# Eleven microseconds planned for weight loads decoded within attention, seven for the first MoE's, and part of two chunks' moves issued by GpSimd

## Chip, cores and metric

The kernel runs on one core of a Trainium2 chip. The metric is the device time of one execution in microseconds (us). A comparison is made with the median of several executions.

## What is computed

Talking-heads attention (scores and attention weights are mixed over the heads, before and after the softmax), then a mixture-of-experts layer with one dense expert and an ELU (the first MoE), then a second one with a SoLU and a layer norm. All weights of both MoEs arrive as 64-bit floats and are used as 32-bit ones.

```python
scores = scale * np.matmul(q, k.transpose(0, 1, 3, 2))      # 4 batches, 12 heads, 448 x 448, head size 64
scores = np.einsum('bhij,hg->bgij', scores, w_pre)
attn = np.exp(scores - np.max(scores, axis=-1, keepdims=True))
attn = attn / (np.sum(attn, axis=-1, keepdims=True) + 1e-09)
attn = np.einsum('bhij,hg->bgij', attn, w_post)
x = np.matmul(attn, v)                                      # 1792 tokens x 768
h = x @ w_in                                                # 768 -> 2048
g = np.where(h > 0.0, h, np.exp(np.minimum(h, 0.0)) - 1.0)
x = g @ w_out                                               # 2048 -> 768
h = x @ w_in2                                               # 768 -> 1024, SoLU, layer norm, 1024 -> 768
```

## The kernel before, in words

**Attention.** A batch's 448 query rows are cut into chunks of up to 12 groups of ten rows (`CH`, 17 chunks in all; the first batch's are 4, 8, 12, 12 and 9 groups). For each chunk PE makes the scores of two heads at a time (L445), ACT or DVE copies them from PSUM into one of eight `sev` buffers (L451), and a DMA, called a move here (`move`, L453), spreads each head's rows into `sp`, where twelve heads of five rows lie on 64 partitions. There is one `sp` buffer for even chunks and one for odd. Two groups of a chunk form a unit; there are 92. A unit is the mixing before the softmax on PE (`pre`, tile `pm`, L515), the row maximum on DVE (L520), the exponential with its sum on ACT (L525), 1/sum on DVE (L529, L532), the weights of the second mixing on GpSimd (L536), that mixing on PE (`post`, tile `po`, L548) and its copy from PSUM on DVE or ACT (L556). At the end of each chunk PE multiplies with v (tile `av`, L597).

**Weights decoded within attention.** The first MoE works on groups of 256 hidden columns (`fg`, eight of them). The weights of group 0 are decoded while attention runs, in 16 pieces of 192 columns (L616 to L664): a load of 64-bit words into `kst` (two buffers), then on DVE the clamp of the high words (L635), on ACT the scaling (L639), on DVE three integer steps (L643, L647, and the join, L652), and a store into `w1s` in DRAM. A piece's load depends on the join of the piece before. Near the end of attention six loads `wy <- w1s` (`add_w`, L683) bring them back and split them.

**What sets the order of attention.** Each operation is an entry of a list with a rank, its engine or engines with a cost each, and what it depends on. `schedule` (L298) works through the list with a clock of its own: an operation may start when each of its inputs is `seen`. That is the input's planned end plus `lag` where a lag is given, and otherwise plus the engine's `tail` and `more`:

```python
            if o.lag is not None:
                return o.end + o.lag
            ...
            return o.end + tail[o.eng] + o.more
```

For a DMA on SP the tail is 2.0, so a `kst` load with `more=.3` counts as landed 2.3 us after its issue, and a `wy` load with `more=.5` after 2.5 us. Where several engines are named, the one that would end first is taken. The clock only sets the order in which instructions are written into each engine's stream. On the chip every stream runs in order, and each instruction waits for its real inputs.

**The first MoE.** For every group `fg` and each of four token blocks `tb`, `hid` makes two halves `ft` (L258), `elu` brings them through DVE, ACT and DVE (L265, L266, L267), and `outp` makes six PSUM tiles `o` in four buffers (L750), which DVE adds to `x1` (L766). The weights of group `fg + 1` and, in what room is left, those of the second MoE (`w2_spill`) are decoded meanwhile. `decode` (L156) gives a piece's stages with the time that must pass before each:

```python
        first = [(0, load, 0), (3.3, hiword, 1, 2), (0, loword, 1), (0, sign, 1), (0, join, 1)]
```

`load` is a 512 KB DMA into `ws` (L163), `hiword` is L172 on DVE and L173 on ACT, `loword`, `sign` and `join` are L177, L182 and L186 on DVE; a split on ACT and GpSimd follows (L189, L190). `tick` (L95) is called behind every half of `hid` and every tile of `outp`, and writes stages whose time has come by a second clock, `clk`, which `spend` moves on. At most three pieces are active, and at most two of them past `load`. `w1_piece(fg, i)` decodes piece `i` of group `fg`; pieces 0 to 2 are of `w_in`, 3 to 5 of `w_out`.

Of the kernel before, what the change touches and what calls it, by code (L numbers as in the profile page):

```python
# [64 lines left out]
def kernel(ctx: ExitStack, tc: tile.TileContext, qa, kt, vt, wpre, wpost,  # L65
# [4 lines left out]
    nc = tc.nc  # L70
# [82 lines left out]
    x_done = [[] for _ in range(NB)]  # L153
    w1, xT, xst_t, wi_t, wo_t = {}, {}, {}, {}, {}

    def decode(src, n, mul=None, dst=None, spill2=None):  # L156

        a = {}

        def load():  # L160
            p = pools["wstg"]
            a["t"] = (p.tile([128, 1024], F32, tag="ws", name="ws", bufs=4)[:, :2 * n],)
            nc.sync.dma_start(out=a["t"][0].bitcast(U64), in_=src)  # L163

        def hiword():
            p = pools["wstg"]
            a["t"] += (p.tile([128, 512], F32, tag="wy", name="wy")[:, :n],
                       p.tile([128, 512], I32, tag="wq", name="wq")[:, :n])
            st, y, q = a["t"]
            a["y"] = y  # L170
            w = st.rearrange("p (n t) -> p n t", t=2)
            nc.vector.tensor_scalar(w[:, :, 1], w[:, :, 1], F64_TOP, -F64_TOP, ALU.min, ALU.max)  # L172
            nc.scalar.activation(out=y, in_=w[:, :, 1], func=AF.Copy, scale=2.0 ** -112)  # L173

        def loword():
            wi = a["t"][0].rearrange("p (n t) -> p n t", t=2).bitcast(I32)
            nc.vector.tensor_scalar(a["t"][2], wi[:, :, 0], 29, None, ALU.logical_shift_right)  # L177

        def sign():
            wi = a["t"][0].rearrange("p (n t) -> p n t", t=2).bitcast(I32)  # L180
            q = a["t"][2]
            nc.vector.scalar_tensor_tensor(q, wi[:, :, 1], -0x80000000, q, ALU.bitwise_and, ALU.bitwise_or)  # L182

        def join():
            y, q = a["t"][1].bitcast(I32), a["t"][2]
            nc.vector.scalar_tensor_tensor(y, y, 3, q, ALU.logical_shift_left, ALU.bitwise_or)  # L186

        def split():
            nc.scalar.copy(dst[0], a["y"])  # L189
            nc.gpsimd.tensor_tensor(dst[1], a["y"], f(dst[0]), ALU.subtract)  # L190

        def split2():
            t = a["t"][0].bitcast(F32R)
            hi, lo = t[:, :n], t[:, n:]
            if mul is not None:
                nc.scalar.mul(a["y"], a["y"], mul)
            nc.scalar.copy(hi, a["y"])
            nc.gpsimd.tensor_tensor(lo, a["y"], f(hi), ALU.subtract)

        def store2():  # L200
            nc.sync.dma_start(out=spill2, in_=a["t"][0])

        first = [(0, load, 0), (3.3, hiword, 1, 2), (0, loword, 1), (0, sign, 1), (0, join, 1)]
        if spill2 is not None:
            return first + [(SD, split2, SW), (1.8, store2, 0)]
        return first + [(SD, split, SW)]
# [4 lines left out]
    def w1_piece(fg, i):  # L211

        m, sl = i // 3, slice((i % 3) * 512, (i % 3) * 512 + 512)
        return decode((wo1 if m else wi1)[fg, :, sl], 512, dst=(w1[fg][2 * m][:, sl], w1[fg][2 * m + 1][:, sl]))

    def xT_alloc(tb, p):
        xT[tb] = (p.tile([128, ECH, S], F32R, name=f"xh{tb}"), p.tile([128, ECH, S], F32R, name=f"xl{tb}"))
# [157 lines left out]
    for u in range(NU):  # L375
# [4 lines left out]
        c = units[u][0]  # L380
# [18 lines left out]
    k_op, q_op, av_op, sc_ev = {}, {}, {}, {}  # L399

    def dma(out, in_, e="sp"):
        (nc.scalar if e == "act" else nc.sync).dma_start(out=out, in_=in_)


    pool("spb")
# [24 lines left out]
    def add_score(c, h):  # L430

        b, _, G = CH[c]
        n = 5 * G
        ring = ("sc", "po", "pm")[h // 2 % 3] if c == 0 else "sc"
        scb, svb = [Buf(ring) for _ in range(2)], [Buf("sev") for _ in range(2)]
        r = t_sc[c, h]
        key = "sc", c, h

        def mm(e):
            T[key] = [pools["ps_" + ring].tile([128, 512], F32, tag=ring, name="sc") for _ in range(2)]  # L440
            q, k = q_t[c, h // 6], kt_t[b, h]
            for x in range(2):
                for i in range(2):
                    sl = slice(64 * i, 64 * i + 64)
                    nc.tensor.matmul(T[key][i][64 * x:64 * x + 64, :S], q[sl, h % 6 // 2, 64 * x:64 * x + 64], k[sl, :],  # L445
                                     start=True, stop=True)

        def evac(e, i):
            t = T["sv", c, h + i] = (k0.tile([128, S], F32, name=f"s0_{h + i}") if c == 0 else
                                     sev_p.tile([128, S], F32, tag="sev", name="sev"))  # L450
            copier(e)(t, T[key][i][:, :S])  # L451

        def move(e, i, p, r0, r1):  # L453
            if c not in sp_t:
                sp_t[c] = sp_t[c - 2]
            dma(sp_t[c][p:p + 13 * (r1 - r0 - 1) + 1:13, 0:G, :], T["sv", c, h + i][r0 * G:r1 * G], e)

        o1 = op(r, mm, [k_op[b, h], q_op[c, h // 6]], scb, [qb_[c, h // 6], kb[b, h]], pe=SC)
        for i in range(2):
            sv = [] if c == 0 else [svb[i]]  # L460
            o2 = sc_ev[c, h + i] = op(r + .9 + .1 * i, lambda e, i=i: evac(e, i), [o1], sv, [scb[i]], act=.54, dve=.62)
            for n, to in enumerate([(h + i, 0, 10)] if h + i < 11 else [(11, 0, 5), (64, 5, 10)]):
                sp_op.setdefault(c, []).append(op(r + 2 + .2 * i + .1 * n, lambda e, i=i, to=to: move(e, i, *to), [o2], [spb_[c]], sv, lag=3.5, sp=.78, **({"act": .78} if c < 2 else {})))

    spb_ = {c: Buf(f"sp{(NC - c) % 2}") for c in range(NC)}
    o = op(7.0, lambda e: dma(wpre_t, wpre), sp=.5)
# [148 lines left out]
    last = None  # L615
    for n in range(16):  # L616
        sl = slice((n % 8) * 192, (n % 8) * 192 + 192)
        src, dst = (wo1 if n > 7 else wi1)[0, :, sl], w1s[n // 8][:, sl]
        t0 = t_pre[first[2]] + 10 + n * (t_pre[first[NC - 1]] - t_pre[first[2]] - 35) / 16
        sb = Buf("kst")  # L620
        key = ("w", n)

        def load(e, key=key, src=src):
            t = kst_p.tile([128, 2, S], F32, tag="kst", name="kst").rearrange("p a b -> p (a b)")
            T[key] = t[:, 0:384], t[:, 384:576], t[:, 576:768].bitcast(I32)
            dma(T[key][0].bitcast(U64), src)

        def words(key=key):
            st, y, q = T[key]
            w = st.rearrange("p (n t) -> p n t", t=2)  # L630
            return w, w.bitcast(I32), y, q

        def clamp(e, words=words):
            w = words()[0]
            nc.vector.tensor_scalar(w[:, :, 1], w[:, :, 1], F64_TOP, -F64_TOP, ALU.min, ALU.max)  # L635

        def scale(e, words=words):
            w, _, y, _ = words()
            nc.scalar.activation(out=y, in_=w[:, :, 1], func=AF.Copy, scale=2.0 ** -112)  # L639

        def loword(e, words=words):
            _, wi, _, q = words()
            nc.vector.tensor_scalar(q, wi[:, :, 0], 29, None, ALU.logical_shift_right)  # L643

        def sign(e, words=words):
            _, wi, _, q = words()
            nc.vector.scalar_tensor_tensor(q, wi[:, :, 1], -0x80000000, q, ALU.bitwise_and, ALU.bitwise_or)  # L647

        def join(e, words=words):
            _, _, y, q = words()  # L650
            y = y.bitcast(I32)
            nc.vector.scalar_tensor_tensor(y, y, 3, q, ALU.logical_shift_left, ALU.bitwise_or)  # L652

        def store(e, key=key, dst=dst):
            dma(dst, T[key][1])

        o = op(t0, load, [last], [sb], sp=.5, more=.3)
        o = op(t0 + 4, clamp, [o], [], [sb], dve=.17)
        oa = op(t0 + 4.5, scale, [o], [], [sb], act=.26)
        o = op(t0 + 5, loword, [o], [], [sb], dve=.17)  # L660
        o = op(t0 + 5.5, sign, [o], [], [sb], dve=.27)
        o = op(t0 + 6, join, [oa, o], [], [sb], dve=.27)
        T["ws", n] = op(t0 + 6.5, store, [o], [], [sb], sp=.5, more=.3)
        last = o  # L664
# [18 lines left out]
    def add_w(i, r):  # L683
        m, sl = i // 3, slice((i % 3) * 512, (i % 3) * 512 + 512)
        wy = Buf("wy")
        key = ("w1", i)

        def load(e):
            T[key] = pools["wstg"].tile([128, 512], F32, tag="wy", name="wy")
            dma(T[key], w1s[m][:, sl])  # L690

        def hi(e):
            copier(e)(w1[0][2 * m][:, sl], T[key])

        def lo(e):
            eng[e].tensor_tensor(w1[0][2 * m + 1][:, sl], T[key], f(w1[0][2 * m][:, sl]), ALU.subtract)

        o = op(r, load, [o_moe] + [T["ws", n] for n in range(8 * m, 8 * m + 8)], [wy], sp=.5, more=.5)
        o = op(r + 4, hi, [o], [], [wy], act=.52, dve=.33)
        return op(r + 5, lo, [o], [], [wy], pool=1.25, dve=.6)  # L700

# [276 lines left out]
```

## Time and profile before

| | |
|---|---|
| median of 3 runs | 1145.31 us (1144.37 to 1147.18) |
| the profiled execution | 1142.14 us |
| its span, first to last instruction | 1140.3 us |
| PE busy | 1078.1 us (95%) |
| DVE, ACT, POOL busy | 735.0 (64%), 502.4 (44%), 246.2 us (22%) |
| DMA, mean over the span | 124 GB/s |
| chain that ended last | PE 63%, DVE 14%, DMA 13%, ACT 4% |

A row of the trace names the line of the kernel, the engine, the operation and its tiles (out<-in). PE is TensorE's matmuls, PEld its weight loads, POOL is GpSimd and SP is SyncE, which here only issues DMAs. The idle time of an engine is put down to what ended it. PEclk is the granted clock of TensorE as a share of full speed. Attention fills the first 392 us, the first MoE runs to 889 us, and the second takes the rest.

### The profile page before, as it was taken

Reading aid. Unit: us, or ns where it says so; the run is one execution under the profiler, and the core shown is the slowest. Engines: PE = TensorE matmul, PEld = TensorE weight load, DVE = VectorE, ACT = ScalarE, POOL = GpSimd, SP = SyncE. Lnnn points to the kernel's source line nnn. Section 1 sums busy time; section 2 is a strip of 40 time slices with the busy share of each in tenths; the row PEclk is TensorE's granted clock in tenths of the full one; section 3 lists DMA queues with packets and bytes.
Section 4 is the critical chain, followed back from the end, with each engine's and each line's share of the span. In section 5 each row is a group of like instructions: output and inputs, shape, how many; then the busy total and the mean of one; then the engine's idle time right before and its main releaser. Section 6 shows DMA issues by size and latency. Waiting matters only on the chain.

```text
span 1140.3 us, 29850 instructions
## 1 busy us (share of the span) xinstructions
PE 1078.1 (95%) x12520; PEld 905.9 (79%) x12520; DVE 735.0 (64%) x1401; ACT 502.4 (44%) x1072; POOL 246.2 (22%) x243
## 2 busy tenths in 40 slices
PE   7789989898999899999998999999999999999998
PEld 2466657666677688989898989989889898988988
DVE  5466668576677837678888778787874554534432
ACT  3466657566666545433333333334342243433422
POOL 2001001010010513434444434344342000000000
PEclk9899999999999899999999999999999999999999
DMA  6665765774753633142425051514135600000001
GB/s 215 185 190 163 214 183 154 216 219 144 224 181 114 200 97 118 68 147 93 148 65 193 16 199 28 177 45 162 60 101 213 240 14 29 28 14 28 15 28 42
DMA packets 80526, 141.76 MB, mean 124 GB/s; under 512 B 20648, under 2 KB 60424, under 8 KB 80392
## 3 DMA queue, kind: packets, MB, share of 16 engines
q1 hardware_dynamic: 79190, 137.99, 37.8%
q8 instruction: 98, 1.61, 0.6%
q10 hardware_dynamic: 1202, 1.87, 0.5%
q14 instruction: 36, 0.29, 0.1%
HBM read 75.96 MB, written 25.17 MB: 89 GB/s over the span
## 4 chain that ended last, share of the span: by engine, by line
PE 63%; DVE 14%; DMA 13%; ACT 4%; issue 3%; SPq 1%; POOL 1%; ACTq 0%; DVEq 0%; POOLq 0%
PE h L258 11%; PE o L750 11%; PE o L893 10%; PE h L846 10%; PE po L548 6%; PE av L597 5%; PE pm L515 5%; PE sc L445 4%; DMA ws<-in_wi_dram 4%; DMA sp<-sev 3%; DMA kst<-in_wo_dram 2%; DVE wy L186 2%; DMA kst<-in_wi_dram 2%; DVE wq L177 2%; DVE x L766 2%
## 5 line engine op out<-in xcount | busy, mean ns | idle before, releaser
L548 PEld LDWEIGHTS po<-wr,e 60*64 60x64 f32 x5760 | 118.5, 139 | 53.0 <-issue 29.8
L750 PE MATMUL o<-gh,woh 128*128 128x448 f32 x384 | 142.5, 371 | 16.7 <-DVE x L766 14.6
L520 DVE TENSOR_REDUCE st<-pm 128x1 f32<-128x448 f32 (+1 forms) x184 | 109.3, 616 | 65.2 <-PE pm L515 64.1
L525 ACT ACTIVATE e<-pm,st 128x448 f32<-128x448 f32 (+1 forms) x184 | 115.6, 633 | 70.4 <-DVE st L520 51.9
L271 POOL TENSOR_TENSOR glo<-g,gh 128x448 fp32r<-128x448 f32 x64 | 86.6, 1353 | 259.6 <-issue 146.2
L750 PE MATMUL o<-glo,woh 128*128 128x448 f32 x384 | 141.4, 368 | 0.0
L750 PE MATMUL o<-gh,wol 128*128 128x448 f32 x384 | 140.9, 367 | 0.0
L548 PE MATMUL po<-wr,e 60*64 60x60 f32 x5760 | 124.7, 224 | 13.0 <-DVE at L556 12.3
L515 PE MATMUL pm<-sp,wpre_t 64*64 64x448 f32 x720 | 110.8, 570 | 21.6 <-ACT e L525 15.7
L445 PE MATMUL sc<-kt,q 64*64 64x448 f32 x816 | 118.9, 566 | 7.2 <-DMA kt<-in_kt_dram 4.4
L893 PE MATMUL o<-w,lh 128*128 128x384 f32 x448 | 120.3, 340 | 0.0
L266 ACT ACTIVATE t<-t 128x448 f32<-128x448 f32 x64 | 37.0, 578 | 161.5 <-DVE t L265 161.5
L536 POOL TENSOR_TENSOR wr<-wpost_t,st 128x120 f32<-128x120 f32 (+1 forms) x91 | 36.6, 403 | 330.9 <-DVE st L532 271.7
L846 PE MATMUL h<-w,x2h 128*128 128x512 f32 x336 | 107.7, 395 | 0.0
L766 DVE TENSOR_TENSOR x<-x,o 128x448 f32<-128x448 f32 x168 | 100.5, 611 | 8.3 <-PE o L750 8.3
L258 PE MATMUL h<-xh,wih 128*128 128x448 f32 x288 | 105.5, 366 | 0.0
L258 PE MATMUL h<-xh,wil 128*128 128x448 f32 x288 | 105.1, 365 | 0.0
L258 PE MATMUL h<-xl,wih 128*128 128x448 f32 x288 | 105.1, 365 | 0.0
L750 PEld LDWEIGHTS o<-gh,woh 128*128 128x128 f32 x384 | 72.7, 189 | 27.2 <-DVE x L766 18.8
L597 PEld LDWEIGHTS av<-at,v 128*64 128x64 f32 x1632 | 76.6, 138 | 15.7 <-ACT e L525 8.2
L597 PE MATMUL av<-at,v 128*64 128x120 f32 (+3 forms) x1632 | 83.5, 260 | 0.5 <-ACT x L604 0.5
L893 PEld LDWEIGHTS o<-w,lh 128*128 128x128 f32 x448 | 81.7, 188 | 0.6
(96 smaller groups left out, 1949.7 us busy)
## 6 DMA issues: line engine op xcount, KB each, us to landing
sp<-sev SPq DMA_DIRECT2D x121, 210.0 KB
ws<-in_wi_dram SPq DMA_DIRECT2D x33, 512.0 KB
ws<-in_wo_dram SPq DMA_DIRECT2D x21, 512.0 KB
sp<-sev SPq DMA_DIRECT2D x44, 157.5 KB
q<-in_qa_dram SPq DMA_DIRECT2D x34, 192.0 KB
v<-in_vt_dram SPq DMA_DIRECT2D x24, 256.0 KB
w2s<-ws SPq DMA_DIRECT2D x12, 512.0 KB
ws<-in_wo_dram SPq DMA_DIRECT2D x16, 384.0 KB
```

The lines of the kernel that those rows point to most:

```text
L258: nc.tensor.matmul(ps[:, :S], a[:, kc * FG + ft * 128:kc * FG + (ft + 1) * 128], x[:, kc, :], start=kc == 0 and n == 0, stop=kc == ECH - 1 ...
L271: nc.gpsimd.tensor_tensor(glo, g, f(gh), ALU.subtract)
L445: nc.tensor.matmul(T[key][i][64 * x:64 * x + 64, :S], q[sl, h % 6 // 2, 64 * x:64 * x + 64], k[sl, :], start=True, stop=True)
L515: nc.tensor.matmul(ps_t[u][r][64 * s:64 * s + 64, :S], wpre_t[sl, :], sp_t[c][sl, g + s, :], start=True, stop=True)
L520: nc.vector.tensor_reduce(out=st_t[u][:P, r:r + 1], in_=ps_t[u][r][:P, :S], op=ALU.max, axis=AX.X, negate=True)
L525: nc.scalar.activation(out=t[:P], in_=ps_t[u][r][:P, :S], func=AF.Exp, bias=st[:P, r:r + 1], scale=1.0, accum_out=st[:P, 2 + r:3 + r])
L548: nc.tensor.matmul(out[:, :, 5 * r:5 * r + 5], e_t[u, r][sl, j:j + 64], wr_t[u][sl, r].rearrange("p (g a) -> p g a", a=5), start=True, sto ...
L597: nc.tensor.matmul(ps[64 * k:64 * k + 64, i, :], v_t[CH[c][0]][:, 6 * n + 2 * i + k, q, :], at_t[c][:, q, 6 * n + 2 * i + k, :w], start=q ...
L750: nc.tensor.matmul(ps[:, :S], a[:, ft * DM + e * 128:ft * DM + (e + 1) * 128], x, start=n == 0, stop=n == 5)
L766: nc.vector.tensor_tensor(x1[tb][:, e, :], x1[tb][:, e, :], ps[:, :S], ALU.add)
L846: nc.tensor.matmul(ps[:, hf * 512:hf * 512 + 512], a[:, k, :], w, start=n == 0, stop=n == 3 * ECH - 1)
L893: nc.tensor.matmul(ps[:, :384], a[:, k, :], w, start=n == 0, stop=n == 3 * FC - 1)
```

## The change

It changes numbers that order the work, and adds an engine to some operations. The `kst` loads of attention now count as landed 11.0 us after their issue (2.3 before), the six `wy` loads after 5.0 us (2.5 before). The three `w_in` pieces of the groups from 2 on wait 7.0 on `clk` between load and `hiword` (3.3 before); pieces of `w_out`, group 1 and the second MoE's weights keep 3.3. The moves of the second and third chunk (`0 < c < 3`) may also be issued by GpSimd, at a planned 1.1 us against SP's 0.78 (and, for the second chunk, ACT's 0.78, as before); `dma` learns of that engine. No computation is added or left out.

```diff
-    def decode(src, n, mul=None, dst=None, spill2=None):
+    def decode(src, n, mul=None, dst=None, spill2=None, land=3.3):
...
-        first = [(0, load, 0), (3.3, hiword, 1, 2), (0, loword, 1), (0, sign, 1), (0, join, 1)]
+        first = [(0, load, 0), (land, hiword, 1, 2), (0, loword, 1), (0, sign, 1), (0, join, 1)]
...
-        return decode((wo1 if m else wi1)[fg, :, sl], 512, dst=(w1[fg][2 * m][:, sl], w1[fg][2 * m + 1][:, sl]))
+        return decode((wo1 if m else wi1)[fg, :, sl], 512, dst=(w1[fg][2 * m][:, sl], w1[fg][2 * m + 1][:, sl]), land=7.0 if fg > 1 and i < 3 else 3.3)
...
     def dma(out, in_, e="sp"):
-        (nc.scalar if e == "act" else nc.sync).dma_start(out=out, in_=in_)
+        {"act": nc.scalar, "pool": nc.gpsimd, "sp": nc.sync}[e].dma_start(out=out, in_=in_)
...
-                sp_op.setdefault(c, []).append(op(..., lag=3.5, sp=.78, **({"act": .78} if c < 2 else {})))
+                sp_op.setdefault(c, []).append(op(..., lag=3.5, sp=.78, **({"act": .78} if c < 2 else {}), **({"pool": 1.1} if 0 < c < 3 else {})))
...
-        o = op(t0, load, [last], [sb], sp=.5, more=.3)
+        o = op(t0, load, [last], [sb], sp=.5, lag=11.0)
...
-        o = op(r, load, [o_moe] + [T["ws", n] for n in range(8 * m, 8 * m + 8)], [wy], sp=.5, more=.5)
+        o = op(r, load, [o_moe] + [T["ws", n] for n in range(8 * m, 8 * m + 8)], [wy], sp=.5, lag=5.0)
```

Since `schedule` draws up one list for all engines, the streams of PE, DVE, ACT, POOL and SP differ almost everywhere in attention from the third chunk's scores on. Three places show what moved.

**SP, around the sixth `kst` load** (`sp<-sev` are moves, `w1s<-kst` the store of a decoded piece, `kst<-in_wi` the next load, `v` and `xs<-x` other transfers). Before:

```order
L402 DMA w1s_91<-kst 128x192
L402 DMA sp<-sev 10x12x448
L402 DMA sp<-sev 5x12x448 x2
L402 DMA v<-in_vt_dram 128x512
L402 DMA xs_59<-x 128x3x88
L402 DMA kst<-in_wi_dram 128x192
```

With the change:

```order
L402 DMA sp<-sev 10x12x448
L402 DMA sp<-sev 5x12x448 x2
L402 DMA w1s_91<-kst 128x192
L402 DMA kst<-in_wi_dram 128x192
L402 DMA v<-in_vt_dram 128x512
L402 DMA xs_59<-x 128x3x88
```

The load now stands right behind the store of the piece before. Over the 15 places of this kind there are one to nine rows between store and load before, and none to three now. On DVE, 10 to 28 instructions lie between the join of one piece (L652) and the clamp of the next (L635) before, and 21 to 30 now.

**DVE, in the first MoE, at the third token block of group 2** (the same in groups 1 to 6: L265 and L267 are the ELU of one half, L172, L177, L182 and L186 one weight piece's decoding, L766 frees one `o` tile). Before:

```order
L265 TENSOR_SCALAR t<-h 128x448
L267 SCALAR_TENSOR_TENSOR g<-t,h 128x448
L172 TENSOR_SCALAR ws<-ws 128x512
L177 TENSOR_SCALAR wq<-ws 128x512
L182 SCALAR_TENSOR_TENSOR wq<-ws,wq 128x512
L186 SCALAR_TENSOR_TENSOR wy<-wy,wq 128x512
L265 TENSOR_SCALAR t<-h 128x448
L267 SCALAR_TENSOR_TENSOR g<-t,h 128x448
L172 TENSOR_SCALAR ws<-ws 128x512
L766 TENSOR_TENSOR x_1_7560<-x_1_7560,o 128x448
```

With the change:

```order
L265 TENSOR_SCALAR t<-h 128x448
L267 SCALAR_TENSOR_TENSOR g<-t,h 128x448
L265 TENSOR_SCALAR t<-h 128x448
L267 SCALAR_TENSOR_TENSOR g<-t,h 128x448
L172 TENSOR_SCALAR ws<-ws 128x512
L766 TENSOR_TENSOR x_1_7560<-x_1_7560,o 128x448
L172 TENSOR_SCALAR ws<-ws 128x512
L766 TENSOR_TENSOR x_1_7560<-x_1_7560,o 128x448
L177 TENSOR_SCALAR wq<-ws 128x512
L766 TENSOR_TENSOR x_1_7560<-x_1_7560,o 128x448
```

The piece that was decoded between the two halves now begins behind the second, and its steps stand between the L766 of that `outp` and the two halves after it. From the next `outp` on the two orders are the same again.

**POOL, at the second and third chunk** (L536 makes a unit's mixing weights). Before, only rows of L536 stand here. With the change:

```order
L402 DMA sp<-sev 10x8x448
L536 TENSOR_TENSOR wr<-wpost_t,st 128x120
L402 DMA sp<-sev 5x12x448
L402 DMA sp<-sev 10x12x448
L536 TENSOR_TENSOR wr<-wpost_t,st 128x120
L402 DMA sp<-sev 10x12x448 x2
L536 TENSOR_TENSOR wr<-wpost_t,st 128x120
L402 DMA sp<-sev 10x12x448
L536 TENSOR_TENSOR wr<-wpost_t,st 128x120 x19
```

Six moves are issued by POOL, one of the second chunk and five of the third; SP keeps eight of the third chunk's thirteen. No other move changes its engine to POOL.

## Rows read from the trace of the kernel before

**Rows 1.** Busy time of each engine by stage (start:end, engines, PEclk, DMA).

```profile
core 0: us, PE busy (x) PEld busy (x) DVE busy (x) ACT busy (x) POOL busy (x), PEclk, DMA share, GB/s
...
18.00:60.00 42.00, 32.79 (x689) 18.61 (x687) 22.05 (x53) 21.67 (x57) 2.71 (x7) 0.92 0.65 194
60.00:360.00 300.00, 277.74 (x7306) 198.49 (x7299) 203.70 (x518) 188.19 (x506) 29.39 (x76) 0.98 0.62 185
...
440.00:890.00 450.00, 433.29 (x2108) 396.84 (x2107) 347.24 (x557) 159.20 (x283) 180.71 (x130) 0.99 0.33 113
890.00:1140.30 250.30, 247.08 (x1285) 223.55 (x1283) 105.37 (x183) 89.13 (x139) 0.00 (x0) 1.00 0.14 50
```

**Rows 2.** What DVE waited for, 60 to 360 us (total us, times, longest).

```profile
DVE kst L635 <- DMA kst<-in_wi_dram: 22.1, 6, 6.4
DVE kst L635 <- DMA kst<-in_wo_dram: 13.3, 5, 5.0
DVE kst L635 <- DMA q<-in_qa_dram: 3.6, 1, 3.6
```

**Rows 3.** What PE waited for, 60 to 360 us.

```profile
PE po L548 <- DVE at L556: 12.3, 6, 2.8
PE pm L515 <- ACT e L525: 9.4, 3, 3.6
```

**Rows 4.** Chain that ended last, around the sixth load (start us, us, what).

```profile
136.27 6.96 DMA kst<-in_wi_dram
...
143.33 0.27 DVE kst L635
...
145.54 1.02 PE pm L515 x3
```

**Rows 5.** Engines by stretch, one with such waits and one without.

```profile
160.00:180.00 20.00, 17.42 (x400) 11.75 (x392) 13.10 (x33) 11.80 (x33) 1.55 (x4) 0.91 0.68 189
180.00:200.00 20.00, 19.98 (x569) 14.83 (x568) 15.30 (x43) 13.87 (x39) 2.32 (x6) 1.00 0.48 147
```

**Rows 6.** PE in order of time, the stops at one place of six groups.

```profile
496.67 0.50 PE L750 MATMUL o<-gh,woh 128*128 128x448 f32 x1 [2.52 <-DVE x L766]
560.28 0.47 PE L750 MATMUL o<-gh,woh 128*128 128x448 f32 x1 [2.68 <-DVE x L766]
622.11 0.48 PE L750 MATMUL o<-gh,woh 128*128 128x448 f32 x1 [2.67 <-DVE x L766]
683.62 0.47 PE L750 MATMUL o<-gh,woh 128*128 128x448 f32 x1 [1.35 <-DVE x L766]
743.45 0.47 PE L750 MATMUL o<-gh,woh 128*128 128x448 f32 x1 [1.33 <-DVE x L766]
803.36 0.47 PE L750 MATMUL o<-gh,woh 128*128 128x448 f32 x1 [1.34 <-DVE x L766]
```

**Rows 7.** Chain that ended last, in the first MoE.

```profile
496.67 4.28 PE o L750 x12
...
548.76 4.90 DMA ws<-in_wi_dram
...
560.28 2.70 PE o L750 x12
...
622.11 3.90 PE o L750 x12
```

**Rows 8.** DVE in order of time, before the stop at 560.28 us.

```profile
553.69 0.91 DVE L172 TENSOR_SCALAR ws<-ws 128x512 f32<-128x512 f32 x1 [1.31 <-DMA ws<-in_wi_dram]
554.52 1.52 DVE L177 TENSOR_SCALAR wq<-ws 128x512 int32<-128x512 int32 x1
556.08 0.69 DVE L182 SCALAR_TENSOR_TENSOR wq<-ws,wq 128x512 int32<-128x512 int32 x1
556.87 0.69 DVE L186 SCALAR_TENSOR_TENSOR wy<-wy,wq 128x512 int32<-128x512 int32 x1
```

**Rows 9.** SP in order of time, moves of the third chunk and behind.

```profile
27.30 7.84 SPq L402 DMA_DIRECT2D sp<-sev  x9
...
39.43 4.59 SPq L402 DMA_DIRECT2D sp<-sev  x4
```

**Rows 10.** PE in order of time, the third chunk's first unit.

```profile
48.91 1.77 PE L515 MATMUL pm<-sp,wpre_t 64*64 64x448 f32 x8 [4.78 <-DMA xs<-x]
```

**Rows 11.** POOL in order of time: its longest instructions.

```profile
0.73 6.86 POOL L474 MEMSET sp<- 128x2688 f32 x2 [0.29 <-POOLq L967]
```

**Rows 12.** ACT in order of time, near the end of attention.

```profile
376.69 0.94 ACT L225 CAST xh<-xst 128x896 fp32r<-128x896 f32 x1 [3.52 <-issue]
```

More of the change, by code (lines that the diff above doesn't have):

```diff
@@ L462, in add_score @@
             for n, to in enumerate([(h + i, 0, 10)] if h + i < 11 else [(11, 0, 5), (64, 5, 10)]):
-                sp_op.setdefault(c, []).append(op(r + 2 + .2 * i + .1 * n, lambda e, i=i, to=to: move(e, i, *to), [o2], [spb_[c]], sv, lag=3.5, sp=.78, **({"act": .78} if c < 2 else {})))
+                sp_op.setdefault(c, []).append(op(r + 2 + .2 * i + .1 * n, lambda e, i=i, to=to: move(e, i, *to), [o2], [spb_[c]], sv, lag=3.5, sp=.78, **({"act": .78} if c < 2 else {}), **({"pool": 1.1} if 0 < c < 3 else {})))
     spb_ = {c: Buf(f"sp{(NC - c) % 2}") for c in range(NC)}
```

## The prediction

> **What bounds the kernel now.** I read the busy time by stage first. TensorE is the engine to watch in every stage, and it is not full in attention or in the first MoE: from 60 to 360 us it works 277.7 of 300 us, from 440 to 890 us 433.3 of 450, while the second MoE has it busy 247.1 of 250.3 us [rows 1]. So no more than some tens of microseconds can be had, all of it in PE's stops and in stretches at a lower granted clock.
>
> Next, who waits for whom between 60 and 360 us. DVE stands still 39.0 us (22.1 + 13.3 + 3.6) in front of L635, the first instruction of a weight piece [rows 2]. PE's own stops in the same stretch come to 21.7 us (12.3 + 9.4), behind a DVE copy and behind an ACT exponential [rows 3]. The chain ties the two together: a `kst` load is issued at 136.27 us and takes 6.96 us, DVE's L635 starts at 143.33, and only after the row maximum and the exponential behind it in their streams does PE go on, at 145.54 [rows 4]. DVE has work for later units behind L635, but its stream is in order. The planner counted the load as landed after 2.3 us; the trace shows 6.96. In a stretch with such a wait PE works 17.42 of 20 us at a granted clock of 0.91; in the next one, without a long wait, 19.98 of 20 at 1.00, with DVE busy 15.30 us [rows 5]. Without these stops PE sets the pace there, not DVE.
>
> In the first MoE, PE stops at one place of each of six groups, for 2.52, 2.68, 2.67, 1.35, 1.33 and 1.34 us, each time for an `o` buffer that DVE had not yet added to `x1` [rows 6]. At the second of them a weight load took 4.90 us [rows 7]; DVE waited 1.31 us for it and then decoded the whole piece, until 557.56 (556.87 + 0.69), before the next half's ELU and the first L766 [rows 8].
>
> **The change part by part.** The sum is made against the profiled execution, 1142.1 us, which lies 3.2 us under the median of 1145.3; I add the 3.2 back at the end.
>
> *The `kst` loads.* Nothing is added: 16 loads, 16 stores and the same 64 DVE and 16 ACT instructions, in another order. By the order of the streams a load now stands at most three rows behind the store of the piece before, and 21 to 30 DVE instructions lie between the two pieces' work. A DVE instruction of this stretch takes 0.39 us (203.7 / 518 [rows 1]), so 8 to 12 us of DVE work alone, and more with its pauses, pass while the load lands; 6.96 us would do. I take the wait as gone. What PE wins is its 21.7 us of stops [rows 3], and the clock: at a mean of 0.98 over 300 us, 6.0 us of full speed are missing [rows 1], and the low stretch is the one with the stop [rows 5]. Together 27.7 us at best. The pauses had also let late moves, evacuations and SP catch up, which no stretch of this trace shows when they are gone for long; the only evidence that nothing replaces them is that the stretch without them has no stop. At worst all of it comes back under another name, so the bounds are 0 and 27.7. I take three quarters, 20.8, nearer the upper end because of that full stretch.
>
> *The first MoE.* In the changed order the piece no longer stands between the two halves: both ELUs come first, then L172 and the first L766 directly. PE's stops of [rows 6] are the wait for this L766. At 560.28 DVE had been late by the wait and the decoding, 1.31 + 0.91 + 1.52 + 0.69 + 0.69 = 5.1 us, some of it overlapped [rows 8]; the stop was 2.68 us, so all of it goes. The decoding is moved to behind the first evacuations, where four `o` buffers lie between DVE and PE and two halves of `hid` follow, in which PE needs nothing from L766. The other pieces are as before from the next `outp` on. I count all six stops, 11.9 us. After two of them PE also ran its next twelve matmuls in 4.28 and 3.90 us instead of 2.70 [rows 7], 2.8 us more. Sum 14.7. At the lowest, DVE's decoding stops PE elsewhere for half as long, 7.
>
> *The moves on GpSimd.* SP issued nine moves back to back in 7.84 us, 0.87 each, and the third chunk's last two in the group that begins at 39.43 [rows 9]; PE then waited 4.78 us for that chunk's first unit [rows 10] (the trace names another transfer, which this unit does not read; a move is what it needs). Five moves less are 4.4 us less for SP. So the gain has an upper bound of 4.8 us plus the clock, 0.08 of 42 us [rows 1], 8.2 in all. The trace of before shows no DMA issued by GpSimd. Its nearest rows for a price are SP's 0.87 and, far off, the two clearings at the start, 6.86 us together [rows 11], of which the one twice as wide would take some 4.6. At 4.6 each the five moves begin near 27.3, end at 50.3 and land about as late behind as before, 9 us later than now. I take 3 us gained, nearer to SP's row, since both only hand over a transfer.
> The Trainium skill ("DMA: Bandwidth & Descriptors", section "Issuing engines are not separate DMA queues") speaks against more: transfers issued by different engines share the same 16 DMA engines, and only issue time is saved. By that rule this term would be at most the 4.4 us of issue; by the wait of [rows 10] and its clock it could be 8.2.
>
> *The `wy` loads.* Near the end of attention ACT stood 3.52 us in front of a copy of `xst` [rows 12], whose planned landing is not changed. I cost this edit at nothing, with 3 us either way.
>
> *Sum:* 20.8 + 14.7 + 3 = 38.5; 1142.1 - 38.5 = 1103.6, and with 3.2 the median is **1107 us**.
>
> **The rivals.**
> *Everything comes back.* No wait replaces the old ones: 27.7 + 14.7 + 8.2 = 50.6, so 1094.7. For it, the full stretch [rows 5]; against it, the pauses hid whatever is late next.
> *Attention gives it back.* The waits of L635 turn into waits for moves, evacuations or `xst`, or SP still issues the loads late: 1142.1 - 14.7 - 3 + 3.2 = 1127.6. For it, DMA engines busy 0.68 of the time in the stretch with waits [rows 5]; against it, they show 0.62 over the stage [rows 1], so there is room to spread.
> *GpSimd issues late.* Its moves hold up its own L536 and the third chunk by the 9 us bounded above: 1107 + 3 + 9 = 1119. Against it, the moves are six in all.
> The Trainium skill ("SBUF — State Buffer", section "SBUF: two separate sides") gives a reason: GpSimd writes descriptors through a port that some DVE instructions lock. No row here shows it.
> *The new order is worse (the other side).* With the decoding spread among the units, DVE's copies at L556 come later than PE needs the next `po` buffer, in every unit. It decides from 38.5 / 92 units = 0.42 us a unit; at 0.6 us the time would be 1107 + 55 = 1162. Against it, PE had no stop while DVE worked 15.30 of 20 us [rows 5], and with the stage shortened DVE's mean becomes 203.7 of 273 us, 0.75, which is less than that.
> *Nothing changes.* The same waits move to the planner's next wrong number in both stages: 1145.
>
> **How the numbers follow.** Forecast (1099 to 1117) 0.52; everything back 0.13; attention gives it back (1118 to 1139) 0.16; GpSimd late 0.08; nothing changes 0.06; worse 0.05. A measurement of this kernel can tell about 0.3% (3.4 us) from no change. The first four are faster, 0.89; same 0.06; slower 0.05. The range leaves out half of the best case, a third of the second rival, and the last two: 1093 to 1130.
>
> **What would show it.** Right: DVE's idle time before L635 under 5 us, PE over 290 of each 300 us in attention, no stop at L750 in groups 1 to 6, the third chunk's first unit earlier by some 3 us. Wrong: new stops on `sp<-sev`, `xst` or `at`; L635 still waiting for `kst`; POOL's moves taking several microseconds each; the first MoE not shorter by some 13 us.

## The result, and the profile after

| | before | changed |
|---|---|---|
| median of 6 runs each | 1147.30 us (1144.37 to 1150.10) | 1120.14 us (1116.97 to 1124.12) |
| ratio, 95% interval | | 0.9766 (0.9738 to 0.9793) |
| the profiled execution | 1142.14 us | 1116.97 us |
| its span | 1140.3 us | 1115.2 us |

The change makes the kernel 27 us faster. 1107 had been forecast, with a range of 1093 to 1130.

The two traces are compared by TensorE's idle time, a stretch's length less its busy time. The first stretch ends at 60 us, the others at the same events in both: at the weighing (L536) of the 84th unit, at the stop of 1.5 us behind ACT's first evacuation of the first MoE (L764; at 449.53 us before, at 437.47 now), and at the first matmul of the second MoE. Busy time by stretch (the columns are those of [rows 1]), before:

```profile
0.00:60.00 60.00, 44.33 (x763) 22.54 (x767) 30.94 (x65) 26.58 (x65) 10.14 (x14) 0.94 0.64 196
60.00:361.21 301.21, 278.94 (x7330) 199.70 (x7323) 204.87 (x523) 188.86 (x507) 29.39 (x76) 0.98 0.62 185
361.21:449.53 88.32, 82.39 (x1094) 70.32 (x1089) 54.24 (x88) 43.62 (x90) 29.77 (x26) 0.96 0.44 137
449.53:889.09 439.56, 424.40 (x2065) 389.03 (x2065) 338.84 (x544) 154.25 (x274) 176.91 (x128) 0.99 0.33 113
```

The same with the change:

```profile
0.00:60.00 60.00, 47.87 (x876) 25.66 (x878) 34.78 (x74) 26.23 (x64) 14.33 (x21) 0.97 0.75 208
60.00:340.86 280.86, 270.62 (x7114) 192.08 (x7110) 201.14 (x516) 185.34 (x497) 29.23 (x76) 1.00 0.66 196
340.86:437.47 96.61, 87.04 (x1188) 73.71 (x1188) 57.83 (x90) 46.55 (x98) 29.07 (x26) 0.95 0.39 125
437.47:863.54 426.07, 421.81 (x2064) 387.85 (x2065) 327.63 (x544) 155.16 (x274) 168.66 (x128) 1.00 0.34 117
```

Up to the first MoE's stop both kernels run the same matmuls (9,168 records each), though not in the same of these stretches: the end of attention has 1,094 of them before and 1,188 with the change. So for attention busy times are compared over all three. Idle time went from 15.67 + 22.27 + 5.93 = 43.87 us to 12.13 + 10.24 + 9.57 = 31.94; busy time stayed, 405.66 and 405.53. Attention won 12.1 us, all of it idle time. The first MoE won 13.5: idle 15.16 to 4.26, busy 424.40 to 421.81. From there on nothing changed (251.2 and 251.7 us). 12.1 + 13.5 - 0.5 = 25.1, the difference of the spans.

The end of attention went the other way: its idle time rose by 3.6 us, with the granted clock at 0.95 (0.96 before). Its lengths, 88.32 and 96.61 us, hold different numbers of matmuls; the last 1,188 before the stop took 91.55 us before and 96.73 now.

DVE no longer waits for `kst`. Its row for L635, with an empty list under what it waited for [rows 2]:

```profile
L635 DVE TENSOR_SCALAR kst<-kst x16: 242/253/286, 58.9 to 315.2; 128x192 f32<-128x192 f32 x16
L635 DVEq EVENT_SEMAPHORE  x6: 21/21/21, 159.2 to 291.7; - x6
its engine sat idle before it (us, times) until:
who waited for it (us, times):
```

What PE waited for between 60 and 341 us (total us, times, longest). The two waits of [rows 3], 12.3 and 9.4 us, are down to nothing and 0.2. What stands there now was, but for 0.2 us of issue at L548 and the last row, not in the list before:

```profile
PE sc L445 <- DMA q<-in_qa_dram: 3.1, 2, 2.8
PE av L597 <- issue: 1.6, 1, 1.6
PE pm L515 <- DMA xs<-x: 1.6, 2, 0.9
PE po L548 <- issue: 1.3, 3, 0.8
PE pm L515 <- DMA q<-in_qa_dram: 0.8, 1, 0.8
...
PE pm L515 <- ACT e L525: 0.2, 1, 0.2
```

PE in the first MoE, its stops at L750 over 0.25 us for DVE. The six of [rows 6] are gone; the one of 0.89 us stands at another place, 72 matmuls ahead of the third of them, where the kernel before had none over 0.25 us. The last of these rows, like 1.74 us at 850.07 before, is for pieces of the second MoE, whose wait was not changed:

```profile
586.17 0.47 PE L750 MATMUL o<-gh,woh 128*128 128x448 f32 x1 [0.89 <-DVE x L766]
805.79 0.47 PE L750 MATMUL o<-gh,woh 128*128 128x448 f32 x1 [0.28 <-DVE x L766]
822.97 0.47 PE L750 MATMUL o<-gh,woh 128*128 128x448 f32 x1 [2.33 <-DVE x L766]
```

The end of attention: PE, ACT, DVE and POOL in order of time.

```profile
360.77 1.02 PE L515 MATMUL pm<-sp,wpre_t 64*64 64x448 f32 x3 [4.81 <-ACT e L525]
...
359.15 0.94 ACT L225 CAST xh<-xst 128x896 fp32r<-128x896 f32 x1 [4.64 <-DMA xst<-xs]
...
357.56 1.38 DVE L225 CAST xh<-xst 128x896 fp32r<-128x896 f32 x1 [1.31 <-DMA xst<-xs]
360.39 2.15 DVE L230 TENSOR_TENSOR xl<-xst,xh 128x896 fp32r<-128x896 f32 x1
362.46 2.57 DVE L696 TENSOR_TENSOR wil<-wy,wih 128x512 fp32r<-128x512 f32 x1
...
360.13 1.47 POOL L696 TENSOR_TENSOR wil<-wy,wih 128x512 fp32r<-128x512 f32 x1
361.56 2.93 POOL L230 TENSOR_TENSOR xl<-xst,xh 128x896 fp32r<-128x896 f32 x1
```

ACT stands 4.64 us in front of a copy of `xst`; the exponentials are behind it in its stream, and PE stops for 4.81. [Rows 12] had the same wait at 3.52, and PE behind it, in the kernel before:

```profile
378.31 1.01 PE L515 MATMUL pm<-sp,wpre_t 64*64 64x448 f32 x3 [3.28 <-ACT e L525]
```

GpSimd's moves, first their durations on POOL (ns, min/median/max, first and last start):

```profile
L402 POOL DMA_DIRECT2D sp<-sev x6: 582/622/761, 13.3 to 40.2; - x6
```

And the DMA issues between 18 and 60 us, the four large moves of POOL (KB each, median us from issue to landing):

```profile
sp<-sev POOLq DMA_DIRECT2D x4, 210.0 KB, 7.3
```

### The profile page after: what moved, and what is told of

The parts are those of the page before. It is cut to its first block, busy times and chain, and to the rows that moved or that the text cites. A ratio compares the mean times of both kernels' runs of the same rounds, so it can differ in the third digit from the quotient of the medians.

```text
span 1115.2 us, 29836 instructions
## 1 busy us (share of the span) xinstructions
PE 1075.3 (96%) x12520; PEld 903.6 (81%) x12520; DVE 727.4 (65%) x1404; ACT 502.5 (45%) x1069; POOL 241.3 (22%) x249
## 5 line engine op out<-in xcount | busy, mean ns | idle before, releaser
L548 PEld LDWEIGHTS po<-wr,e 60*64 60x64 f32 x5760 | 119.7, 137 | 39.1 <-issue 28.7
L750 PE MATMUL o<-gh,woh 128*128 128x448 f32 x384 | 142.2, 370 | 5.8 <-DVE x L766 3.7
L750 PE MATMUL o<-glo,woh 128*128 128x448 f32 x384 | 140.7, 366 | 0.0
L750 PE MATMUL o<-gh,wol 128*128 128x448 f32 x384 | 140.3, 365 | 0.0
L271 POOL TENSOR_TENSOR glo<-g,gh 128x448 fp32r<-128x448 f32 x64 | 83.6, 1307 | 231.5 <-issue 134.3
L548 PE MATMUL po<-wr,e 60*64 60x60 f32 x5760 | 124.9, 221 | 3.7 <-DVE at L556 1.5
L766 DVE TENSOR_TENSOR x<-x,o 128x448 f32<-128x448 f32 x168 | 101.3, 610 | 8.6 <-PE o L750 8.6
L536 POOL TENSOR_TENSOR wr<-wpost_t,st 128x120 f32<-128x120 f32 (+1 forms) x92 | 36.1, 392 | 298.7 <-DVE st L532 214.2
L750 PEld LDWEIGHTS o<-gh,woh 128*128 128x128 f32 x384 | 72.5, 189 | 15.1 <-DVE x L766 7.0
```

Source lines behind the costliest of these rows:

```text
L271: nc.gpsimd.tensor_tensor(glo, g, f(gh), ALU.subtract)
L548: nc.tensor.matmul(out[:, :, 5 * r:5 * r + 5], e_t[u, r][sl, j:j + 64], wr_t[u][sl, r].rearrange("p (g a) -> p g a", a=5), start=True, sto ...
L750: nc.tensor.matmul(ps[:, :S], a[:, ft * DM + e * 128:ft * DM + (e + 1) * 128], x, start=n == 0, stop=n == 5)
L766: nc.vector.tensor_tensor(x1[tb][:, e, :], x1[tb][:, e, :], ps[:, :S], ALU.add)
```

## The experiments

Each kernel was timed in rounds against the kernel before, four kernels on one chip. A ratio is to the kernel before on the same chip.

| kernel | median us | ratio | 95% interval |
|---|---|---|---|
| kst lag alone | 1129.56 | 0.9859 | 0.9829 to 0.9889 |
| first MoE alone | 1129.53 | 0.9868 | 0.9840 to 0.9896 |
| GpSimd's moves alone | 1146.85 | 1.0003 | 0.9979 to 1.0027 |
| change, wy lag undone | 1114.65 | 0.9736 | 0.9707 to 0.9764 |
| the change again | 1118.40 | 0.9753 | 0.9725 to 0.9782 |
| wy undone, q later | 1112.09 | 0.9703 | 0.9674 to 0.9731 |
| wy undone, xst later | 1113.08 | 0.9711 | 0.9684 to 0.9738 |
| change, kst 7.0 | 1108.52 | 0.9664 | 0.9638 to 0.9690 |
| change, kst 9.0 | 1117.85 | 0.9736 | 0.9710 to 0.9761 |
| change, kst 5.0 | 1122.04 | 0.9764 | 0.9741 to 0.9788 |
| kst 7.0, wy undone, xst later | 1109.48 | 0.9652 | 0.9626 to 0.9678 |
| kst 7.0, second MoE later too | 1149.86 | 1.0016 | 0.9995 to 1.0038 |

### The parts alone

**The `kst` lag alone**, on the kernel before:

```diff
-        o = op(t0, load, [last], [sb], sp=.5, more=.3)
+        o = op(t0, load, [last], [sb], sp=.5, lag=11.0)
```

> The kernel before with the new lag of the kst loads alone (11.0). Theory A (the waits at L635 were what stopped TensorE in attention, and what is left of the gain is lost at the end of attention to the loads of xst): DVE's 39 us in front of L635 fall under 5, the 80th unit's L536 starts 18 to 25 us earlier than before, the end of attention gives 5 to 10 of it back, time 11 to 17 us under the kernel before. Rival B (the gain of attention came from the moves issued by GpSimd and the order that they brought, not from the loads): time within 5 us of the kernel before. Rival C (the end gives back what the six wy loads planned later push aside): without them here the end keeps it, time 20 to 25 us under before.

16 us were won. DVE has no wait at L635, the 80th unit's L536 starts at 324.30 us (344.54 before), 20.2 us earlier, and the first MoE's stop behind L764 lies at 434.99, 14.5 us earlier, so 5.7 are given back on the way. From the 84th unit to that stop it takes 95.59 us, with 9.03 idle. So theory A's numbers hold, and B and C fall: without the other edits the end of attention is as long as with them. A's reason for the end, the loads of `xst`, is not shown: ACT waits only 0.85 us before its copy there, and PE's longest stop in this stretch is 1.80 us:

```profile
355.25 0.94 ACT L225 CAST xh<-xst 128x896 fp32r<-128x896 f32 x1 [0.85 <-issue]
```

**The first MoE alone**, on the kernel before: `land=7.0 if fg > 1 and i < 3 else 3.3` for the pieces, as in the change.

> The kernel before with the 7.0 between load and L172 for the first MoE's w_in pieces alone. Theory A: the six stops at L750 go, attention stays as it was, time 10 to 15 us under the kernel before. Rival (the stops went because the pieces were shifted against the chip's loads by what attention gained, not by their new place): the stops stay, time within 4 us of before.

15 us were won. The stop behind L764 lies at 449.80 us, as before (449.53), and from there to the second MoE it takes 426.66 us instead of 439.56. All six stops are gone. This part stands on its own, at 12.9 us of the trace. (Without this edit the same stretch took 437.67 and 443.36 us in the other two runs on the kernel before, so it is known to some 3 us.)

**GpSimd's moves alone**, on the kernel before: the two edits of `dma` and `sp_op`.

> The kernel before with the moves issued by GpSimd alone. Theory A: the third chunk begins 2 to 4 us earlier, L635 waits as before (some 39 us), the gain does not last or is 3 us at most: time 0 to 3 us under before. Rival B (these moves brought most of attention's gain): 10 us or more under before, and L635 waits less.

No difference. The eighth unit's L536 comes at 56.10 us instead of 60.81, but at the 24th the lead is gone (126.43 and 124.67): DVE still waits 24.6 + 16.1 us at L635, and PE stops behind it. The longest of these stops, and the wait just ahead of it:

```profile
71.68 0.27 DVE L635 TENSOR_SCALAR kst<-kst 128x192 f32<-128x192 f32 x1 [6.36 <-DMA kst<-in_wi_dram]
...
72.56 1.87 PE L548 MATMUL po<-wr,e 60*64 60x60 f32 x59 [4.49 <-DVE at L556]
```

**The `wy` lag undone**, on the changed kernel:

```diff
-[wy], sp=.5, lag=5.0)
+[wy], sp=.5, more=.5)
```

> The changed kernel with the wy loads' lag as before (more=.5). Until some 350 us the streams are those of the changed kernel. Theory A (the end of attention loses some 8 us because the loads of xst are late, whose planned landing is not changed): the wait for xst stays, time within 3 us of the changed kernel. Rival C (the wy lag pushes other work aside): the 4.81 us stop of TensorE near 361 us goes, time 5 to 9 us under the changed kernel, near 1112.

The stop of 4.81 us is gone, as rival C had it; ACT still waits for `xst`, 1.16 us, and PE's longest stop there is 1.91. The idle time of the end falls from 9.57 to 6.90 us, but the clock there is 0.93 and the stretch takes 95.47 us instead of 96.61. The ratios, 0.9736 and 0.9766, have overlapping intervals. This lag costs somewhere from nothing to some 7 us; the runs don't settle it.

```profile
358.49 0.94 ACT L225 CAST xh<-xst 128x896 fp32r<-128x896 f32 x1 [1.16 <-DMA xst<-xs]
```

### What the end of attention, and the rest of the idle time, hang on

The next four ran on one chip, the change itself among them.

> The changed kernel once more, on the chip of the three that follow, so that they can be held against it. About 27 us under the kernel before; the stops near 81 us (2.8 us, for q) and near 361 us (4.8 us, for xst) are there again. If the wy loads' new lag costs what the run without it suggested, this one is 3 to 6 us slower than the runs built on that one.

0.9753, as the first time (0.9766). The stops for `q` (3.26 us at 79.52) and for `xst` (4.55 us at 364.34) are there again. One length differs between the two profiled executions of this same kernel: from 60 us to the 84th unit 284.96 us here, with 12.47 idle, against 280.86 with 10.24. Differences of 4 us in this stretch say nothing, then. The end is steadier, 97.52 and 96.61 us. PE's busy time up to the first MoE's stop differs too, by 3.1 us (408.59 and 405.53) for the same matmuls. The next two runs have the `wy` lag undone and are 6.3 and 5.3 us faster than this one, near the 3 to 6 expected if that lag costs time; but each has one more edit, and the intervals overlap.

**q later**, on the change with the `wy` lag undone:

```diff
-        q_op[c, hf] = op(..., load, [], [qb_[c, hf]], sp=.5, more=.5)
+        q_op[c, hf] = op(..., load, [], [qb_[c, hf]], sp=.5, lag=4.5)
```

> The changed kernel with the wy lag as before, and the loads of q counted as landed 4.5 us after their issue (2.5 before). Theory A (what is left of TensorE's idle time between 60 us and the last chunk is the same fault at other loads, q first: 3.1 + 0.8 us): the stop near 80 us goes, the stretch from 60 us to the 84th unit's L536 is 2 to 4 us shorter, time 2 to 4 us under the run without the wy lag (near 1111). Rival D (another wait follows each that is taken away, since TensorE's units are one chain through DVE and ACT): the time stays within 1.5 us of it.

The wait for `q` fell to one of 1.39 us, but from 60 us to the 84th unit it takes 285.92 us (282.21 with the `wy` lag undone alone), and PE's idle time in it is the same (10.38 and 10.41). Three waits for moves (`sp<-sev`), 7.3 us over the whole kernel and one of them, 1.76 us, in this stretch, and one of 2.1 us put down to issue, stand among PE's waits. Theory A misses in the stretch; the total is 3.8 us less by the ratios than without this edit (0.9703 and 0.9736), but their intervals overlap.

**xst later**, on the same kernel: in `add_x`, `lag=7.0` in place of `more=1.0`.

> The changed kernel with the wy lag as before, and the loads of xst counted as landed 7.0 us after their issue (3.0 before). Theory A (the end of attention waits for xst): from the 84th unit's L536 to TensorE's stop at the first MoE's first evacuation (ACT L764, 1.5 us) 3 to 6 us less than the 95.5 us of the run without the wy lag, time 3 to 6 us under it. Rival E (DVE's and GpSimd's copies and subtractions of xst and wy themselves hold up the units there, whatever their order): within 1.5 us of it.

The end of attention takes 91.16 us, 4.3 less, as theory A had it, and ACT's copy no longer waits. The way from 60 us to the 84th unit took 4.1 us more than in the run without this edit, with the same streams, and the total (0.9711 and 0.9736) shows no clear gain.

**kst 7.0**, on the change: `lag=7.0` for `lag=11.0`.

> The changed kernel with 7.0 in place of 11.0 for the kst loads, 0.04 us over the longest landing in the rows of before (6.96). Theory A (what counts is that the planned landing covers the real one): most of L635's waits stay away, under 8 us in all, time within 4 us of the changed kernel. Rival F (the slack beyond the landing is what helps, because SP issues the loads late behind moves): L635 waits 10 us or more, time 5 to 12 us over the changed kernel.

Both missed: one wait of 3.3 us is left at L635, and the time is 10 us under the change (0.9664 against 0.9753; the intervals don't touch). Where it comes from:

```profile
60.00:342.53 282.53, 270.03 (x7148) 195.55 (x7146) 204.31 (x519) 184.60 (x494) 29.09 (x75) 0.99 0.65 196
342.53:430.32 87.79, 83.55 (x1173) 70.27 (x1169) 55.66 (x90) 45.17 (x96) 27.56 (x27) 1.00 0.44 137
430.32:855.47 425.15, 421.08 (x2065) 386.65 (x2065) 328.13 (x544) 155.07 (x274) 167.88 (x128) 1.00 0.34 117
```

The stretch with the 16 pieces is as long as with 11.0 (282.53, against 280.86 and 284.96). The end is not: 87.79 us against 96.61 (88.79 against 96.73 for the last 1,188 matmuls), with 4.24 us of idle time against 9.57 and the clock at 1.00. Over all of attention PE's busy time is 401.73 us instead of 405.53 for the same matmuls, little more than the 3.1 us between two executions of the change. DVE here makes all three copies of the first `xst` tiles, and nothing of `xst` stands in ACT's stream until 367.85 us:

```profile
355.53 0.62 DVE L225 CAST xh<-xst 128x896 fp32r<-128x896 f32 x1
...
359.51 2.03 DVE L225 CAST xh<-xst 128x896 fp32r<-128x896 f32 x2 [0.46 <-DMA xst<-xs]
...
367.85 0.95 ACT L225 CAST xT<-xst 128x896 fp32r<-128x896 f32 x1
```

### Is it the lag, or the order of the end?

> The changed kernel with 9.0 for the kst loads. Theory G (above the real landing each us more of planned wait only moves the 16 pieces later, since each load waits for the piece before, and the last of them into the end of attention): time between the two known ones, 1111 to 1116, the last L635 between 295 and 315 us. Rival H (the 10 us between 7.0 and 11.0 are the luck of one order of the end): no relation, anywhere from 1106 to 1122, and the difference lies in the end of attention behind the 84th unit.

> The changed kernel with 5.0 for the kst loads, under the longest landings but over the 2.3 of before. Theory A (the planned landing has to cover the real one): L635 waits again for some of its loads, 8 to 20 us in all, and TensorE behind it; time 4 to 12 us over the run with 7.0 (1113 to 1121). Rival (any lag that spreads the piece's work will do): L635 waits under 5 us, time within 3 us of the run with 7.0.

| lag of kst | waits at L635 us | last L635 at | 60 us to 84th unit (idle) | the end (idle) | ratio |
|---|---|---|---|---|---|
| 5.0 | 19.4 | 298.1 | 285.25 (13.11) | 97.64 (10.89) | 0.9764 |
| 7.0 | 3.3 | 295.3 | 282.53 (12.50) | 87.79 (4.24) | 0.9664 |
| 9.0 | 3.9 | 313.0 | 284.42 (12.57) | 96.45 (9.69) | 0.9736 |
| 11.0 | 0 | 315.2 | 280.86 (10.24) | 96.61 (9.57) | 0.9766 |
| 11.0, again | 0 | 319.3 | 284.96 (12.47) | 97.52 (9.48) | 0.9753 |

Theory G falls: with 5.0 the last piece is as early as with 7.0, and the end is the longest of all. Rival H holds: the end decides, and with these lags it takes either 88 us or 97. In the long ones ACT makes one of the three copies, and waits for its load. With 9.0 and with 5.0:

```profile
363.18 0.94 ACT L225 CAST xh<-xst 128x896 fp32r<-128x896 f32 x1 [5.07 <-DMA xst<-xs]
```

```profile
364.90 0.94 ACT L225 CAST xh<-xst 128x896 fp32r<-128x896 f32 x1 [5.98 <-DMA xst<-xs]
```

The waits at L635 came back with 5.0 as theory A had it, and by the ratios the time is some 11.5 us over that with 7.0 (13.5 by the medians, which are of two chips), but 9.9 of the traces' difference lie in the end and only 2.7 in the stretch with the pieces, less than the 4 us that say nothing there. There 19.4 us of DVE's waiting, the longest 4.7, went with 13.11 us of PE's idle time, little over the 10.24 and 12.47 of the change, which has no such wait; before, 39.0 us, the longest 6.4, went with 22.27. That PE feels the long waits alone would fit this, but no run separates their length from their number.

**kst 7.0, the wy lag undone and xst later**, together:

> The changed kernel with 7.0 for the kst loads, the wy lag as before and 7.0 for the loads of xst: the parts that were each faster, together. If they add up (some 10 us for the first, 5 for the other two): 1103 to 1106. If the end of attention is already cured by the first (its idle time behind the 84th unit is 4.2 us there): 1106 to 1110.

1109.48: the second case. The end takes 87.62 us with 4.67 idle. Here ACT does make copies, at 360.96 and 366.78, and waits for neither load. So the short end comes with ACT's copies as well as without them.

ACT's wait is not the whole of the long ends either. The run with `xst` later and a `kst` lag of 11.0 differs from this one in that lag alone; no copy of ACT waits in it, and yet its end takes 91.16 us, with PE stopping 3.01 us behind an exponential. And with the `wy` lag undone, or with the `kst` lag alone, the end takes 95.5 us with ACT's waits at 1.16 and 0.85 us. What else makes these ends long stays open.

**kst 7.0, and the second MoE's pieces later too**: the default of `land` set to 7.0, which `w2_spill` takes.

> The changed kernel with 7.0 for the kst loads, and the 7.0 between load and L172 for the second MoE's pieces too. Theory A (the last stop of the first MoE, 2.3 us near 816 us, is of the same kind as the six): it goes, 1 to 3 us under the run with 7.0, near 1106. Rival: the second MoE's pieces come later through the decoding, and those left over at the end of the first MoE stop TensorE there: 2 to 10 us over it.

All 40 us are lost again, in the first MoE: 465.91 us instead of 425.15, with 36.73 us of idle time against 4.06. PE's longest stop, what DVE waited for, and the longest of its waits for the first MoE's own pieces:

```profile
882.01 0.74 PE L750 MATMUL o<-gh,woh 128*128 128x448 f32 x1 [16.35 <-DVE x L766]
```

```profile
DVE ws L172 <- DMA ws<-in_wo_dram: 47.0, 8, 7.7
```

```profile
602.78 0.43 DVE L172 TENSOR_SCALAR ws<-ws 128x512 f32<-128x512 f32 x1 [6.46 <-DMA ws<-in_wo_dram]
```

At most three pieces are active, and a piece that waits for its load keeps its place. With 7.0 for them fewer of the second MoE's are decoded along the way: L172 of their sixteenth piece of 384 columns comes at 875.4 us instead of 815.5. The rest is written out at once in `drain`, in the last group, where two L172 in a row wait 6.35 and 6.37 us, for loads issued 3.6 and 3.7 us ahead of them. The rival's 2 to 10 us were far too small, and it saw only the end: five of the eight waits, 26.6 us, are for `w_out` pieces of the first MoE (128x512), whose own number is still 3.3, and 11 to 15 us behind each of them PE stops, for 4.00, 2.68, 1.72, 1.71 and 1.49 us. Why these loads came so late is not shown.

## Why the prediction was right, and where not

The direction, the range and the two main mechanisms were right: the waits at L635 and the six stops went. The time fell 13 us short of the likeliest number; 2.0 of these are not the change's, since the median of the kernel before rose from 1145.3 (three runs) to 1147.3 (six). Against that the gain is 27.2 us of 38.5.

- **First MoE, 14.7 forecast: 13.5 in the trace** (10.9 idle, 2.6 clock). The run with this part alone shows it to be independent of the rest.
- **The `kst` loads, 20.8 forecast, and GpSimd's moves, 3: 12.1 for attention as a whole.** The waits at L635 went to zero, and with them both waits of [rows 3], as said. The step that failed is "I take three quarters, 20.8". Two parts of the 27.7 were mis-sized. Of the 22.27 us idle between 60 us and the last units 10.24 remain, so 12.0 came: there are now waits for `q` and others that were not in the list before. And of the 6.0 us of clock nothing came in the sum: the stretch itself went from 0.98 to 1.00 and all of attention from 0.97 to 0.98, but PE's busy time for the same matmuls stayed (405.66 and 405.53). A part of this lies at the end, where the last 1,188 matmuls took 87.16 us of busy time instead of 85.61; why the rest did not show is open. The run with 7.0 had 3.9 us less busy time than before, little over the 3.1 us between two executions of the change. The end of attention, for which the sum had nothing, gave back 3.6 us by its idle time.
- **GpSimd's moves.** The price was right (0.62 us on POOL, near SP's 0.87 and far from 4.6), the rival of late issues did not come about, and the gain was wrong: alone they win nothing (1.0003), since the third chunk's lead is lost by the 24th unit, with L635 still waiting. With the change PE's unit stop of [rows 10] is gone, but the second chunk's units come later (a stop of 3.78 us for a move at 31.14, against 1.14 us at 31.01 before), and the third chunk's first L536 starts at 54.57, not before the 53.79 of before. Idle time up to 60 us fell by 3.5 us.
- **The `wy` loads**, counted at nothing with 3 us either way, lie between nothing and some 7 us of cost.
- **"Attention gives it back"**, the rival at 1127.6, named `xst` as a place to which the waits would turn. It does, in part; the time lies between this case and the forecast. By the prediction's own division 1120 is in this rival's part (1118 to 1139, 0.16) and not in the forecast's (1099 to 1117, 0.52): the range held because it took in two thirds of this rival.
- **Worse order at L556**: PE's waits there for DVE are down to nothing between 60 and 341 us.

Of the signs named: L635 under 5 us, the six stops, POOL's short moves and 13 us in the first MoE came true. PE over 290 of 300 us did not (285.6 from 60 to 360), nor the third chunk 3 us earlier. Of the signs of being wrong one came in part: PE has longer stops than before for `sp<-sev` (3.78 us) and behind ACT's wait for `xst` (4.81).

Shown by runs: the gain of the first MoE; that `kst` alone brings attention's gain; that GpSimd's moves alone bring none; that of the lags tried the three whose order has ACT's copy waiting at the end of attention take 8 to 9 us more there than 7.0 does, by itself or with later `xst`. Not shown: that ACT's wait is what makes the end long (three runs have a longer end than with 7.0 with little of that wait or none), and how the 8 to 9 us split between it, DVE's slow instructions there, the lower clock and the rest of the order. Not settled: what the `wy` lag costs. The two parts alone multiply to 0.9729, close to the change with that lag undone (0.9736), which would fit a small cost.

## What to carry to other kernels

In a stream that is laid out by a planner, a landing time that is too short puts a waiting instruction in front of work that is ready, and one that is too long for everything starves a pipeline with few places: set it per transfer from the trace's landings. When one such number is mended, the next wrong one decides, so look for it in the stage behind, and try two or three values: the outcome here went by the order that came out at the end of a stage, not smoothly with the number. Time parts alone before adding them up: of four edits two made the whole gain, and a better value of one was worth another 1%.

## What the hardware showed

DVE's subtraction L696 takes 0.68 us where GpSimd is idle (at 383.02 us), and 2.57 us at 362.46 us, where GpSimd's subtraction of `xst` ran from 361.56 to 364.49; L230 takes 1.09 us, in the median, and 2.15 at 360.39, beside GpSimd's L696. DVE's ends (365.03 and 362.54 us) lie behind GpSimd's (364.49 and 361.60). The Trainium skill ("SBUF — State Buffer", section "SBUF: two separate sides") says that some instructions of the two engines lock a port that they share, so that one waits for the other; these rows agree. The lock did not show in the moves that GpSimd issued: all six took 0.58 to 0.76 us.
